# Fused attention and gated layer on one core: Q and K of the last batch by casting transfers from GpSimd, transposed in 64x64 quarters

## The chip, the cores and the metric

The kernel runs on one core of a Trainium2 chip. A core has five engines that run side by side, each working through its own instructions in order: TensorE (PE, matrix products and transposes, with PEld its weight loads), VectorE (DVE), ScalarE (ACT), GpSimd (POOL) and SyncE (SP, which here only issues transfers). Sixteen DMA engines move data between the memory of the device and the on-chip buffers. The metric is device time in microseconds (us) of one execution; a time is the median of the runs shown. One further execution is taken by the hardware profiler, and all lines of profiles and traces below come from such an execution.

## The reference

Batch 8, 8 heads, 576 positions, head dimension 64; everything float32. Attention has a causal mask and a decay bias made of a running sum, and its output goes through a gated layer with a causal convolution of five taps (`x` is the attention output with its heads side by side, `xp` the same with four rows of zeros ahead):

```python
scores = scale * np.matmul(q, k.transpose(0, 1, 3, 2))
s_pos = np.maximum(s, 0.0)
cum = np.cumsum(s_pos, axis=-1)
bias = -(cum[:, :, :, None] - cum[:, :, None, :])
scores = np.where(causal, -1000000000.0, scores + np.minimum(bias, 0.0))
...
attn = np.exp(scores)
attn = attn / (np.sum(attn, axis=-1, keepdims=True) + 1e-09)
return np.matmul(attn, v).astype(np.float32)
...
for k in range(K):
    gate_pre += conv_w[k][None, None, :] * xp[:, k:k + S, :]
gate = 1.0 / (1.0 + np.exp(-gate_pre))
val = x @ w_val
return (gate * val @ w_out).astype(np.float32)
```

## The kernel before

The work is cut into 32 units n = 4 b + p: batch b (0 to 7) and pair p of heads (0 to 3). One unit goes through these steps, each named in the kernel by a short word and the unit's number:

- `s0`, `s1`, `s2`: scores of the pair in blocks (PE, line 506), each followed by its exponential `e0`, `e1`, `e2` (ACT, line 557). `s4`, `e4` do the last 64 positions for a whole batch.
- `mk`: for some units the causal mask of the diagonal blocks, on POOL (line 580); for the others PE does it.
- `vp`: the values of a pair times their decay weights, on POOL (line 475), from the loaded values `vst`.
- `av0`, `av`: the weighted sums of the two heads, PE (line 595). They read the masked exponentials and `vp`'s result. Then `rec`, `nm` (DVE) divide, `xt` (PE) transposes, `xe` copies out.
- `p2` to `p4`, `t1` to `t4`: the convolution taps (POOL lines 655 and 674, DVE, some on ACT), `th` the tanh (ACT), `val` and `out` the two products of the layer (PE, lines 704 and 724), `glu`, `oe` on DVE and ACT, `st` the store (SP).

Q and K come in once a batch, in two halves. In spite of its name, `ld_q.b` brings heads 0 to 3 of both Q and K, and `ld_k.b` heads 4 to 7 of both. Each is two transfers of 512 KB, one of Q and one of K (line 436), into a float32 buffer `qkf`: an even partition 2x holds rows 8x to 8x+7 of Q for four heads, the odd one beside it the same rows of K. `c_q.b` and `c_k.b` (line 374, POOL in most batches) cast a half to bfloat16 into one of three buffers `qkb` and change the order within a partition from (head, row, d) to (row, head, d), so that two heads of a row lie side by side. `qq.b.0` and `qq.b.1` (PE, line 630) then transpose a half in 32 pieces of 64 partitions by 128 columns (two heads), which land in two banks of PSUM with the two heads in the two halves of the partitions; `qe` copies them to `QKT`, from which the scores are formed. Tails of 64 positions come separately (`ld_t`, `tt`, `te`).

No scheduler decides the order. A table, `ORDER`, written out by hand, lists every step as `name:engine:buffers`; the program records the steps in that order, each on the named engine, so each engine's own order is the order of its entries. Semaphores between engines are set by the data and the buffers. An engine whose next instruction has to wait holds back everything behind it.

Around the change the table stands in batches 4 and 5 of attention: units 16 to 20, while Q and K of batches 6 and 7 are brought in. `ld_q.7` uses `qkf` buffer 4 and `ld_k.7` buffer 2, both issued by SP; `c_q.7:G:2` and `c_k.7:G:0` (G is POOL) cast them into `qkb` buffers 2 and 0. `qq.7.0` and `qq.7.1` stand later, among units 21 to 23.

Of the kernel before, what the change touches and what calls it, by code (L numbers as in the profile page):

```python
# [245 lines left out]
xe.16:A s1.18:T:3+4 glu.12.1:V val.13.0:T:7 ld_k.7:S:2 e4.5.3:A glu.12.0:V mk.18:G t1.16:V:0 val.13.1:T:6 e1.18:A  # L246
s2.18:T:1+2 glu.13.1:V vp.5.0:G val.15.0:T:0 e2.18:A t3.16:V s0.19:T:3+4:2 val.15.1:T:6 glu.13.0:V st.0.8:S th.15:A:4
vp.5.1:G t4.16:V av0.18:T:1+2 ld_t.7:S e0.19:A av.18:T glu.15.1:V c_q.6:G:1 rec.18:V s1.19:T:6+7 glu.15.0:V
s2.19:T:3+4 e1.19:A nm.18:V out.1.4:T:0 t2.16:V e2.19:A xt.18:T:1 ld_v.6.0:S vp.5.3:G s0.20:T:6+7:1 xe.18:V tt.6:T:5
e0.20:A oe.1.4:V:1 qq.6.1:T:4:3 mk.19:G t1.18:V:2 th.16:A:1 st.1.3:S av0.17:T:6+7 te.6:V av.17:T qe.6.3:A c_q.7:G:2  # L250
ld_v.6.3:S qq.6.0:T:0:2 rec.17:V qe.6.2:A nm.17:V out.1.6:T:5 t3.18:V qe.6.0:A ld_v.6.4:S av0.19:T:6+7 p2.18:G:1
oe.1.6:V:5 s2.20:T:3+4 xt.17:T:0 e2.20:A t4.18:V mk.20:G av.19:T ld_v.6.2:S out.1.5:T:5 xe.17:V qe.6.1:A rec.19:V
t2.18:G t1.17:V:1 s0.21:T:3+4:0 oe.1.5:A:0 nm.19:V s1.20:T:1+2 st.1.5:S out.1.8:T:5 c_k.7:G:0 e1.20:A ld_v.6.1:S
t2.17:V xt.19:T:6 e0.21:A st.1.2:S out.1.7:T:7 t4.17:V st.1.1:S oe.1.8:A:4 vp.5.2:G xe.19:V s2.21:T:3+4 s1.21:T:1+2
t3.17:V e2.21:A val.16.0:T:5 t1.19:V:3 p3.19:G:0 val.16.1:T:0 ld_v.7.3:S e1.21:A val.17.0:T:3 glu.16.0:V ld_v.7.4:S
glu.16.1:V val.18.0:T:4 p4.19:G:1 th.17:A:2 st.1.4:S t2.19:V s0.22:T:0+1:2 qq.7.0:T:2:5 e0.22:A st.1.6:S glu.17.0:V
t4.19:G val.18.1:T:6 qe.7.0:V val.17.1:T:3 ld_v.7.2:S th.18:A:3 av0.21:T:0+1 oe.1.7:A:0 mk.22:G glu.18.1:V av.21:T
qe.7.1:A ld_v.7.0:S glu.17.1:V s0.23:T:6+7:0 glu.18.0:V t3.19:G s2.22:T:2+3 rec.21:V ld_v.7.1:S e0.23:A av0.20:T:4+5
nm.21:V av.20:T st.1.7:S e2.22:A vp.6.3:G s4.6.3:T:6+7 rec.20:V xt.21:T:0 nm.20:V val.19.0:T:1 th.19:A:0 vp.6.1:G
s1.22:T:2+3 e4.6.3:A glu.19.0:V val.19.1:T:4 e1.22:A xe.21:V xt.20:T:1 glu.19.1:V p3.21:G:1 s1.23:T:6+7 xe.20:V  # L260
p4.21:A:0 s2.23:T:4+5 out.2.2:T:2 t1.20:V:0 e1.23:A vp.6.2:G t1.21:V:1 out.2.1:T:3 e2.23:A t3.20:V vp.6.0:G
qq.7.1:T:6:7 oe.2.1:A:3 t2.21:V av0.22:T:4+5 oe.2.2:A:2 st.2.1:S av.22:T t4.20:V qe.7.3:A t3.21:G out.2.3:T:0 rec.22:V
t2.20:V qe.7.2:A s0.26:T:2+3:1 t4.21:G nm.22:V tt.7:T:1 th.20:A:4 out.2.0:T:6 te.7:V e0.26:A vp.7.0:G oe.2.3:V:1
xt.22:T:7 oe.2.0:A:5 s2.26:T:4+5 xe.22:V s0.24:T:2+3:2 st.2.3:S e2.26:A av0.23:T:0+1 st.2.0:S t1.22:V:2 p4.22:G:1
av.23:T st.2.2:S e0.24:A st.1.8:S s0.25:T:4+5:0 rec.23:V p2.22:G:0 nm.23:V e0.25:A s1.24:T:2+3 t3.22:V xt.23:T:6
mk.24:G e1.24:A s1.25:T:0+1 xe.23:V s2.24:T:4+5 val.20.0:T:7 t2.22:G t1.23:V:3 e1.25:A val.21.0:T:2 glu.20.0:V
val.21.1:T:3 th.21:A:1 t2.23:V val.20.1:T:7 t4.22:G e2.24:A glu.21.0:V s2.25:T:0+1 glu.21.1:V val.22.0:T:2 e2.25:A
t3.23:V vp.7.2:G s1.26:T:4+5 val.22.1:T:3 glu.20.1:V th.22:A:2 t4.23:V av0.25:T:0+1 vp.7.1:G e1.26:A av.25:T
glu.22.0:V s0.27:T:6+7:0 rec.25:V glu.22.1:V e0.27:A s2.27:T:4+5 vp.7.3:G nm.25:V av0.26:T:2+3 av.26:T e2.27:A
xt.25:T:6 mk.27:G rec.26:V av0.24:T:0+1 nm.26:V xe.25:A av.24:T th.23:A:3 p4.25:G:0 t1.25:V:0 s4.7.3:T:4+5 s1.27:T:2+3  # L270
e4.7.3:A val.23.0:T:7 rec.24:V t2.25:V e1.27:A xt.26:T:4 val.23.1:T:5 nm.24:V t4.25:G xe.26:A av0.27:T:2+3 glu.23.1:V
p3.25:A:1 xt.24:T:0 t1.26:V:1 av.27:T xe.24:A out.2.8:T:1 t3.25:G glu.23.0:V p4.26:A:0 t1.24:V:2 out.2.5:T:7
oe.2.8:A:0 rec.27:V t4.26:G t2.24:V th.25:A:0 u0.28:T:5+6:1 oe.2.5:A:3 nm.27:V out.2.6:T:1 f0.28:A p4.24:G:1 st.2.5:S
t3.24:V xt.27:T:7 oe.2.6:A:1 u1.28:T:2+3 u0.29:T:5+6:2 chk0:V xe.27:A st.2.6:S out.2.7:T:1 f1.28:A t1.27:V:3 t4.24:G
out.2.4:T:0 f0.29:A t2.26:V oe.2.7:A:5 val.25.0:T:2 p2.27:G:0 oe.2.4:A:2 t3.27:V av.28.0:T:3 st.2.7:S th.24:A:1
u1.29:T:4+5 st.2.8:S u0.30:T:0+1:0 glu.25.0:V st.2.4:S p3.26:G:1 val.24.0:T:6 t4.27:V f0.30:A val.24.1:T:2 rec.28.0:V
# [5 lines left out]
xe.30.0:A glu.26.1:V u3.29:T:6+7 u2.30:T:4+5:1 t1.30.0:V:3 f3.29:A out.3.2:T:2 t3.29.0:G rec.31.0:V rec.28.1:V
t2.30.0:V f2.30:A out.3.1:T:6 ml.29:G nm.31.0:V oe.3.2:A:4 p4.30.0:G:1 t3.30.0:V xt.31.0:T:7 th.28.0:A:3 st.3.2:S
u3.30:T:2+3 xe.31.0:V p4.29.0:G:0 u2.31:T:4+5:2 f3.30:A nm.28.1:V av.29.1:T:0 t1.31.0:V:1 ml.30:G val.28.0:T:1 f2.31:A
t4.30.0:G rec.29.1:V t3.31.0:V xt.28.1:T:2 val.30.0:T:3 glu.28.0:V xe.28.1:A t4.29.0:G oe.3.1:A:3 av.30.1:T:4
nm.29.1:V p2.28.1:A:1 t4.31.0:V st.3.1:S val.29.0:T:0 th.30.0:A:1 p4.28.1:G:0 t1.28.1:V:0 th.29.0:A:0 t2.31.0:V
u3.31:T:5+6 t2.28.1:G out.3.3:T:1 f3.31:A rec.30.1:V glu.29.0:V t4.28.1:G nm.30.1:V th.31.0:A:4 xt.29.1:T:7 ml.31:G
val.31.0:T:0 glu.30.0:V xe.29.1:A t3.28.1:V xt.30.1:T:4 p3.29.1:G:1 av.31.1:T:3 glu.31.0:V xe.30.1:A th.28.1:A:2
out.3.0:T:2 t1.30.1:V:3 t1.29.1:V:2 rec.31.1:V t3.30.1:V t3.29.1:G out.3.4:T:0 oe.3.0:A:1 nm.31.1:V p2.30.1:G:0
t2.29.1:V oe.3.3:A:5 xt.31.1:T:2 t4.30.1:V out.3.6:T:3 xe.31.1:A t4.29.1:V st.3.3:S t2.30.1:G oe.3.4:A:0 t1.31.1:V:1  # L290
# [4 lines left out]
"""


def main_path(ctx, tc, q, k, v, s, moe_w_val, moe_conv_w, moe_w_out, out, okcnt):
# [129 lines left out]
    def ld_qk(which):  # L428
        def f(e, b, part=None):
            if b == 0:  # L430
                e.dma_start(out=first[part][which],
                               in_=(q, k)[which][0, HP[part], 0:512, :].rearrange("h (p j) d -> p h (j d)", j=4))
                return
            f, hs = halfof(which, b, part)
            for w, src in enumerate((q, k)):
                e.dma_start(out=f.rearrange("(x w) (h e) -> w x h e", w=2, h=4)[w, :, hs],  # L436
                               in_=src[b, 4 * which:4 * which + 4, 0:512, :][hs].rearrange("h (x j) d -> x h (j d)",
                                                                                          j=8))
        return f
# [401 lines left out]
```

## Time and profile before

| what | value |
|---|---|
| median of 3 runs | 190.05 us (189.24 to 191.22) |
| the profiled execution: its own time | 190.71 us |
| its span, first to last instruction | 189.0 us |
| engine busy: PE, DVE, ACT, POOL | 171.9, 164.2, 171.1, 163.6 us |
| POOL casts of a half of Q and K, 128x2048 | 1.89 us each |
| transposes at line 630, all batches from 1 on | 448, PE busy 9.0 us |
| moved by the DMA engines | 40.46 MB, mean 214 GB/s |

The span covers the engines' instructions; the 1.7 us between it and the execution's own time lie around it. Busy times of different engines overlap, since they run side by side. A matmul shows some 190 ns because its pipeline is long, but many are in flight; how fast they follow each other is read from the start times of groups. Instructions that issue transfers are not counted as busy.

### The profile page before, as it was taken

To read this page: it belongs to the slowest core of one execution; us is meant where nothing else is said; L and a number is where in the kernel's file an instruction comes from. 1 tells how busy PE (TensorE), PEld (TensorE's weight loads), DVE (VectorE), ACT (ScalarE), POOL (GpSimd) and SP (SyncE) were. 2 spreads that over 40 slices of the span, in tenths; PEclk is the share of its full clock that TensorE was granted. 3 is DMA by queue.
4 is the path that set the end of the run, shared out by engine and by line. 5 is a ranking of instruction groups with operands and counts; after the bars stand their busy time and mean duration, and the time that the engine had idled before them with its cause. 6 is when DMAs were issued, how large, how long until landed. Compare 5 with 4: busy or idle time off the path is not lost.

```text
span 189.0 us, 6654 instructions
## 1 busy us (share of the span) xinstructions
PE 171.9 (91%) x2720; PEld 113.4 (60%) x2720; DVE 164.2 (87%) x321; ACT 171.1 (91%) x231; POOL 163.6 (87%) x148
## 2 busy tenths in 40 slices
PE   6898785889999998999888999999999999999991
PEld 2556563277747765576564667486566865776560
DVE  4475999669998899999899899998989899999980
ACT  2789899879999999999979998999999999999772
POOL 5467999699999899999969999999999989899620
PEclk9999998799999999999999999999999999999999
DMA  5999889899999999998799999999132003401164
GB/s 176 272 280 267 229 293 207 215 330 343 275 197 342 269 296 252 329 315 223 167 232 260 351 395 231 175 305 249 63 132 93 3 0 114 169 5 55 61 222 173
DMA packets 62283, 40.46 MB, mean 214 GB/s; under 512 B 47333, under 2 KB 49381, under 8 KB 62250
## 3 DMA queue, kind: packets, MB, share of 16 engines
q1 hardware_dynamic: 61706, 39.49, 75.4%
q8 instruction: 22, 0.36, 0.9%
q10 hardware_dynamic: 544, 0.52, 0.8%
q14 instruction: 11, 0.09, 0.2%
HBM read 30.57 MB, written 9.44 MB: 212 GB/s over the span
## 4 chain that ended last, share of the span: by engine, by line
PE 49%; ACT 14%; SPq 13%; DVE 9%; DMA 6%; issue 5%; POOL 2%; ACTq 0%; DVEq 0%; POOLq 0%
PE bank L724 12%; PE bank L704 11%; PE bank L595 10%; ACT P L557 9%; PE bank L506 7%; SPq L472 4%; PE bank L627 3%; SPq L436 3%; DMA vst<-in_v_dram 3%; DMA first<-in_k_dram 3%; PE bank L630 3%; DVE glu L713 3%; ACT th L691 2%; DVE gp L671 2%; DVE xn L614 2%
## 5 line engine op out<-in xcount | busy, mean ns | idle before, releaser
L557 ACT ACTIVATE P<-bank 128x1024 bf16<-128x1024 f32 x84 | 82.9, 1042 | 5.1 <-PE bank L506 3.8
L671 DVE SCALAR_TENSOR_TENSOR gp<-bank,cwr,gp 128x574 f32<-128x574 bf16 (+6 forms) x72 | 52.5, 743 | 0.4
L674 POOL TENSOR_TENSOR gp<-gp,pr 128x572 f32<-128x572 f32 (+6 forms) x36 | 44.9, 1256 | 6.2 <-DVE gp L671 3.3
L475 POOL TENSOR_TENSOR Vp<-vst,w 128x650 bf16<-128x650 f32 x32 | 40.5, 1283 | 2.9 <-DMA vst<-in_v_dram 1.9
L506 PE MATMUL bank<-QKT 64*128 64x128 bf16 (+4 forms) x592 | 38.0, 239 | 4.9 <-ACT P L557 2.2
L704 PE MATMUL bank<-xT,wv 128*128 128x288 bf16 (+2 forms) x256 | 38.5, 287 | 1.0 <-ACT P L557 0.5
L595 PE MATMUL bank<-Vp,P 128*128 128x65 bf16 x960 | 36.0, 194 | 3.2 <-POOL Vp L475 1.0
L595 PEld LDWEIGHTS <-P 128*128 128x128 bf16 x960 | 33.1, 98 | 7.6 <-issue 3.0
L724 PE MATMUL bank<-wo,glu 128*128 128x512 bf16 x144 | 35.8, 380 | 0.2 <-DVE glu L713 0.2
L506 PEld LDWEIGHTS <-QKT 64*128 64x128 bf16 x592 | 19.7, 95 | 22.7 <-issue 15.4
L655 POOL TENSOR_TENSOR pr<-xT,cwr 128x572 f32<-128x572 bf16 (+6 forms) x28 | 28.2, 1015 | 1.6 <-DVE xT L374 0.9
L713 DVE SCALAR_TENSOR_TENSOR glu<-th,bank 128x288 bf16<-128x288 f32 (+2 forms) x64 | 27.7, 447 | 1.9 <-ACT th L691 0.9
L704 PEld LDWEIGHTS <-wv 128*128 128x128 bf16 x256 | 22.4, 97 | 10.9 <-issue 4.8
L614 DVE TENSOR_TENSOR xn<-bank,recs 128x640 bf16<-128x640 f32 (+2 forms) x36 | 26.9, 746 | 0.6
L666 DVE SCALAR_TENSOR_TENSOR gp<-xT,cwr,bank 128x576 f32<-128x576 bf16 (+2 forms) x36 | 26.4, 741 | 0.7
L374 ACT COPY QKT<-bank 128x1024 bf16<-128x1024 bf16 (+1 forms) x26 | 24.1, 970 | 2.6 <-PE bank L490 2.3
L580 POOL TENSOR_SCALAR_AFFINE_SELECT P<-P 128x1024 bf16<-128x1024 bf16 (+1 forms) x22 | 21.3, 972 | 3.9 <-ACT P L557 3.9
L691 ACT ACTIVATE th<-gp,cwr 128x576 f32<-128x576 f32 x28 | 22.0, 792 | 0.2 <-DVE gp L671 0.2
L724 PEld LDWEIGHTS <-glu 128*128 128x128 bf16 x144 | 12.3, 98 | 13.1 <-issue 1.6
L374 ACT COPY ot<-bank 128x512 f32<-128x512 f32 x26 | 15.2, 608 | 1.8 <-PE bank L724 1.0
L627 PE MATMUL bank<-ident,xn 128*128 128x128 bf16 x164 | 15.2, 223 | 0.5 <-ACT P L557 0.3
L608 DVE RECIPROCAL recs<-bank 128x10 f32<-128x10 f32 (+2 forms) x36 | 7.5, 209 | 8.4 <-PE bank L595 7.8
(66 smaller groups left out, 183.3 us busy)
## 6 DMA issues: line engine op xcount, KB each, us to landing
out_dram<-ot SPq DMA_DIRECT2D x36, 256.0 KB, 4.0
vst<-in_v_dram SPq DMA_DIRECT2D x28, 256.0 KB, 5.7
first<-in_q_dram SPq DMA_DIRECT2D x6, 512.0 KB, 4.5
first<-in_k_dram SPq DMA_DIRECT2D x6, 512.0 KB, 6.0
qkf<-in_q_dram SPq DMA_DIRECT2D x6, 512.0 KB, 7.3
qkf<-in_k_dram SPq DMA_DIRECT2D x6, 512.0 KB, 7.3
vst<-in_v_dram SPq DMA_DIRECT2D x15, 128.0 KB, 5.3
first<-in_q_dram SPq DMA_DIRECT2D x4, 256.0 KB, 4.8
```

The costliest lines, as they stand in the source:

```text
L374: (act.copy if e is act else e.tensor_copy)(dst, src)
L475: e.tensor_tensor(Vps[b % 2][:, :, HP[p]], vslot(b)[:, :, HP[p]], w[:, :, b * 8 + 2 * p:b * 8 + 2 * p + 2].unsqueeze(3).to_broadcast([128, ...
L506: pe.matmul(ps[:, hh, c0:c0 + nq], QKTs[b % 2][r, 1, p, k0:k0 + 128], QKTs[b % 2][r, 0, p, q0:q0 + nq], **kw)
L557: act.activation(out=Pt(n)[:, :, step * 512:(step + 1) * 512], in_=pair((f"s{step}", n)), func=AF.Exp, scale=0.125)
L595: pe.matmul(ps[:, o:o + 65], lhsT, Vps[b % 2][:, kb, 2 * p + w, :], start=(kb == 0), stop=(kb == qb))
L614: vec.tensor_tensor(xns[b % 2][:, g, p * 128:(p + 1) * 128].rearrange("t g (w d) -> t w g d", w=2), ps[:, :, :, 0:64], recs[:, n, :, g].un ...
L655: pool.tensor_tensor(pr, xTs[b % 2][:, c, 4 + lo - m:4 + hi - m], r.to_broadcast([128, hi - lo]), ALU.mult)
L671: vec.scalar_tensor_tensor(gp[:, lo:hi], xps(n, *h)[:, lo - m:hi - m], r, gp[:, lo:hi], ALU.mult, ALU.add)
L674: pool.tensor_tensor(gp[:, lo:hi], gp[:, lo:hi], prs[at[f"p{m}", n, *h][0]][:, lo:hi], ALU.add)
L704: pe.matmul(ps, wv[:, dc, c * 128:(c + 1) * 128], xTs[b % 2][:, dc, 4 + lo:4 + hi], start=(dc == 0), stop=(dc == 3))
L713: vec.scalar_tensor_tensor(glu2[:, c, o + lo:o + hi], th[:, lo:hi], 1.0, ps, ALU.add, ALU.mult)
L724: pe.matmul(bank_of(u, i), glu2[:, c, i * 128:i * 128 + 128], wo[:, c, :], start=(c == 0), stop=(c == 3))
```

## The change

For batch 7 alone, the two halves of Q and K are no longer loaded by SP as float32 and cast by POOL. POOL itself issues four transfers (two for each half) that read float32 and write bfloat16 straight into `qkb`. Steps `c_q.7` and `c_k.7` are gone, and so are SP's four transfers. The transfer leaves the order within a partition as it was loaded, (head, row, d), so two heads of a row no longer lie side by side; for these two halves the transposes take pieces of 64 partitions by 64 columns (one head), 64 of them a half where there were 32.

```diff
-t4.12:V vp.4.1:G s2.17:T:1+2 ld_q.7:S:4 out.1.3:T:3 e2.17:A rec.16:V t3.12:V c_k.6:G:0 th.13:A:0 nm.16:V s0.18:T:1+2:1
+t4.12:V vp.4.1:G s2.17:T:1+2 out.1.3:T:3 e2.17:A rec.16:V t3.12:V c_k.6:G:0 ld_q.7:G:2 th.13:A:0 nm.16:V s0.18:T:1+2:1
...
@@ def ld_qk
-            f, hs = halfof(which, b, part)
+            f, hs = (qkb(which, b), slice(0, 4)) if e is pool else halfof(which, b, part)
...
@@ def qk_T2(e, b, h):
+        if (h, b) in by_pool:
+            src = qkb(h, b).rearrange("p (m j d) -> p m j d", m=4, j=8)
+            for p in range(2):
+                for j in range(8):
+                    for r in range(2):
+                        rows = slice(64 * r, 64 * r + 64)
+                        for hh in range(2):
+                            pe.transpose(row_bank(b, h, r)[64 * hh:64 * hh + 64, p * 512 + j * 64:p * 512 + j * 64 + 64],
+                                         src[rows, 2 * p + hh, j, :], ident[rows, rows])
+            return
...
@@ the loop over ORDER
+    by_pool = set()
...
+                if e == "G":
+                    key = ("qkb", "qk".index(f[3]), ix[0])
+                    by_pool.add(key[1:])
```

In the table, `ld_q.7:G:2` now stands right behind `c_k.6`, and `ld_k.7:G:0` behind `qq.6.1` and ahead of `mk.19`; all other entries keep their order.

On POOL, from `c_k.6` to `c_k.7`, before the change. In these rows `qkb0`, `qkb1` and `qkb2` are the three bfloat16 buffers, `Vp` is written by `vp`, `P` by the masks (the first `P1` row is unit 18, `P2` unit 19, the second `P1` row unit 20), `pr` and `gp` belong to the taps:

```order
L374 CAST qkb0_102<-first_91 128x4x8x64
L475 TENSOR_TENSOR Vp0_109<-vst0_92,w_140 128x5x130
L580 AFFINE_SELECT P1_117<-P1_117 128x2x512
L475 TENSOR_TENSOR Vp1_110<-vst1_93,w_140 128x5x130 x2
L374 CAST qkb1_103<-first_91 128x4x8x64
L475 TENSOR_TENSOR Vp1_110<-vst1_93,w_140 128x5x130
L580 AFFINE_SELECT P2_118<-P2_118 128x2x512
L374 CAST qkb2_104<-qkf2_138 128x4x8x64
L655 TENSOR_TENSOR pr1_135<-xT0_113,cwr_144 128x574
L580 AFFINE_SELECT P1_117<-P1_117 128x2x512
L674 TENSOR_TENSOR gp2_121<-gp2_121,pr1_135 128x574
L374 CAST qkb0_102<-qkf0_136 128x4x8x64
```

The same place of POOL after the change (line numbers differ by a few, since the file grew and the table shrank by a line):

```order
L373 CAST qkb0_102<-first_91 128x4x8x64
L435 DMA qkb2_104<-in_q_dram 64x4x512
L435 DMA qkb2_104<-in_k_dram 64x4x512
L474 TENSOR_TENSOR Vp0_109<-vst0_92,w_140 128x5x130
L579 AFFINE_SELECT P1_117<-P1_117 128x2x512
L474 TENSOR_TENSOR Vp1_110<-vst1_93,w_140 128x5x130 x2
L373 CAST qkb1_103<-first_91 128x4x8x64
L474 TENSOR_TENSOR Vp1_110<-vst1_93,w_140 128x5x130
L435 DMA qkb0_102<-in_q_dram 64x4x512
L435 DMA qkb0_102<-in_k_dram 64x4x512
L579 AFFINE_SELECT P2_118<-P2_118 128x2x512
L664 TENSOR_TENSOR pr1_135<-xT0_113,cwr_144 128x574
```

The first pair of issues stands ahead of the mask of unit 18, the second ahead of the mask of unit 19; the two casts stood behind both masks and are gone.

On SP, before the change, the four loads among stores of the output (`out_0`) and the tails of batch 7 (`tail1`); `first` is the buffer of `ld_q.6`:

```order
L436 DMA first_91<-in_k_dram 64x4x512
L459 DMA tail0_105<-in_q_dram 64x8x64
L459 DMA tail0_105<-in_k_dram 64x8x64
L732 DMA out_0_dram<-ot1_129 128x512
L436 DMA qkf2_138<-in_q_dram 64x4x512
L436 DMA qkf2_138<-in_k_dram 64x4x512
L732 DMA out_0_dram<-ot5_133 128x512
L436 DMA qkf0_136<-in_q_dram 64x4x512
L436 DMA qkf0_136<-in_k_dram 64x4x512
L732 DMA out_0_dram<-ot0_128 128x512
L459 DMA tail1_106<-in_q_dram 64x8x64
```

And after it:

```order
L435 DMA first_91<-in_k_dram 64x4x512
L458 DMA tail0_105<-in_q_dram 64x8x64
L458 DMA tail0_105<-in_k_dram 64x8x64
L741 DMA out_0_dram<-ot1_129 128x512
L741 DMA out_0_dram<-ot5_133 128x512
L741 DMA out_0_dram<-ot0_128 128x512
L458 DMA tail1_106<-in_q_dram 64x8x64
```

The stores and the tails behind the four loads move up; nothing else on SP changes. ACT and DVE keep their rows. PE has 128 rows more, all in `qq.7.0` and `qq.7.1`.

More of the change, by code (lines that the diff above doesn't have):

```diff
@@ L247 @@
[L247 to L276, printed above, removed]
@@ L282 @@
[L282 to L286, printed above, removed]
@@ L292 @@
-oe.3.6:A:2 out.3.5:T:1 glu.29.1:V t3.31.1:V st.3.6:S glu.30.1:V val.31.1:T:0 th.31.1:A:1 outa.3.8:T:7 oe.3.5:A:4
-glu.31.1:V chk:V out.3.8:T st.3.5:S outa.3.7:T:0 oe.3.8:A:3 out.3.7:T st.3.8:S cnt:T:7 oe.3.7:A:5 cntc:V st.3.7:S
-flag:S
+xe.16:A s1.18:T:3+4 glu.12.1:V val.13.0:T:7 e4.5.3:A glu.12.0:V mk.18:G t1.16:V:0 val.13.1:T:6 e1.18:A s2.18:T:1+2
+glu.13.1:V vp.5.0:G val.15.0:T:0 e2.18:A t3.16:V s0.19:T:3+4:2 val.15.1:T:6 glu.13.0:V st.0.8:S th.15:A:4 vp.5.1:G
+t4.16:V av0.18:T:1+2 ld_t.7:S e0.19:A av.18:T glu.15.1:V c_q.6:G:1 rec.18:V s1.19:T:6+7 glu.15.0:V s2.19:T:3+4 e1.19:A
@@ new lines @@
+nm.18:V out.1.4:T:0 t2.16:V e2.19:A xt.18:T:1 ld_v.6.0:S vp.5.3:G s0.20:T:6+7:1 xe.18:V tt.6:T:5 e0.20:A oe.1.4:V:1
+qq.6.1:T:4:3 ld_k.7:G:0 mk.19:G t1.18:V:2 th.16:A:1 st.1.3:S av0.17:T:6+7 te.6:V av.17:T qe.6.3:A ld_v.6.3:S
+qq.6.0:T:0:2 rec.17:V qe.6.2:A nm.17:V out.1.6:T:5 t3.18:V qe.6.0:A ld_v.6.4:S av0.19:T:6+7 p2.18:G:1 oe.1.6:V:5
+s2.20:T:3+4 xt.17:T:0 e2.20:A t4.18:V mk.20:G av.19:T ld_v.6.2:S out.1.5:T:5 xe.17:V qe.6.1:A rec.19:V t2.18:G
+t1.17:V:1 s0.21:T:3+4:0 oe.1.5:A:0 nm.19:V s1.20:T:1+2 st.1.5:S out.1.8:T:5 e1.20:A ld_v.6.1:S t2.17:V xt.19:T:6
```

51 lines of the change are left out of this document (40 added, 11 removed).

## The prediction

> **What bounds the kernel now.** I read the page first, then busy time by stretch, the chain of waits, and at the place of the change the timelines of POOL, PE and SP. The engines' line and the stretches (busy us of PE, PEld, DVE, ACT and POOL with instruction counts, granted clock, DMA share, GB/s):
>
> ```profile
> PE 171.9 (91%) x2720; PEld 113.4 (60%) x2720; DVE 164.2 (87%) x321; ACT 171.1 (91%) x231; POOL 163.6 (87%) x148
> 105.00:120.00 15.00, 14.69 (x265) 9.87 (x263) 14.03 (x28) 14.31 (x19) 14.81 (x13) 1.00 1.08 305
> 120.00:138.00 18.00, 17.96 (x289) 11.81 (x289) 16.71 (x31) 17.77 (x24) 17.13 (x14) 1.00 0.71 188
> 138.00:150.00 12.00, 11.53 (x196) 8.17 (x195) 10.99 (x22) 11.96 (x15) 11.92 (x11) 1.00 0.25 90
> ```
>
> All four working engines are nearly full from 105 to 150 us, so the order of handovers decides, not one engine's load. The chain that ended last, around the two batch-7 transposes (start, length, what):
>
> ```profile
> 120.04 1.02 PE bank L724 x4
> ...
> 124.81 0.33 PE bank L506 x8
> 125.14 0.47 PE bank L630 x32
> ...
> 134.30 0.57 PE bank L630 x32
> ...
> 137.91 0.90 ACT P L557
> ```
>
> From 120 to 138 us the chain runs through PE, the two groups of 32 transposes (`qq.7.0`, `qq.7.1`) among it; at 137.9 it passes to ACT, which in 138 to 150 is busy 11.96 of 12 us. Time added to PE here has no idle time to vanish in.
>
> POOL, from `c_k.6` on. The rows are `c_k.6`, `vp.4.2`, the mask of unit 18, two `vp`, `c_q.6`, `vp.5.3`, the mask of unit 19, `c_q.7`; later `c_k.7`, `vp.5.2` and a tap of unit 19:
>
> ```profile
> 103.21 1.89 POOL L374 CAST qkb<-first 128x2048 bf16<-128x2048 f32 x1
> 105.06 1.28 POOL L475 TENSOR_TENSOR Vp<-vst,w 128x650 bf16<-128x650 f32 x1
> 106.29 1.10 POOL L580 TENSOR_SCALAR_AFFINE_SELECT P<-P 128x1024 bf16<-128x1024 bf16 x1
> 107.35 2.53 POOL L475 TENSOR_TENSOR Vp<-vst,w 128x650 bf16<-128x650 f32 x2
> 109.81 1.90 POOL L374 CAST qkb<-first 128x2048 bf16<-128x2048 f32 x1
> 111.66 1.29 POOL L475 TENSOR_TENSOR Vp<-vst,w 128x650 bf16<-128x650 f32 x1
> 112.90 1.10 POOL L580 TENSOR_SCALAR_AFFINE_SELECT P<-P 128x1024 bf16<-128x1024 bf16 x1
> 113.94 1.90 POOL L374 CAST qkb<-qkf 128x2048 bf16<-128x2048 f32 x1
> ...
> 119.53 1.89 POOL L374 CAST qkb<-qkf 128x2048 bf16<-128x2048 f32 x1
> ...
> 125.20 1.40 POOL L674 TENSOR_TENSOR gp<-gp,pr 128x572 f32<-128x572 f32 x1 [0.34 <-DVE gp L671]
> ```
>
> No gap stands in POOL from 103 to 116 us. What PE does with POOL's results, in its own timeline: `av0.18` and `av.18`, then `qq.6.1`, `qq.6.0`, `av0.19`; and `qq.7.0` and `qq.7.1`, each with the group behind it:
>
> ```profile
> 109.01 1.07 PE L595 MATMUL bank<-Vp,P 128*128 128x65 bf16 x30
> ...
> 113.07 0.64 PE L630 MATMUL bank<-ident,qkb 64*128 64x64 bf16 x32
> 113.73 1.07 PE L595 MATMUL bank<-Vp,P 128*128 128x65 bf16 x30
> 114.73 0.64 PE L630 MATMUL bank<-ident,qkb 64*128 64x64 bf16 x32
> ...
> 116.18 0.61 PE L595 MATMUL bank<-Vp,P 128*128 128x65 bf16 x15
> ...
> 124.98 0.63 PE L630 MATMUL bank<-ident,qkb 64*128 64x64 bf16 x32
> 125.54 1.15 PE L704 MATMUL bank<-xT,wv 128*128 128x288 bf16 x8
> ...
> 134.24 0.64 PE L630 MATMUL bank<-ident,qkb 64*128 64x64 bf16 x32
> 134.81 1.08 PE L595 MATMUL bank<-Vp,P 128*128 128x65 bf16 x30
> ```
>
> **The casts.** Two go: 1.90 + 1.89 = 3.79 us of POOL. Nobody waited for them: `c_q.7` ended at 115.84 and is read at 124.98, `c_k.7` at 121.42 and 134.24. In 95 to 150 us POOL itself waits, and is waited for, this much (total, times, longest):
>
> ```profile
> POOL gp L674 <- DVE gp L671: 2.2, 4, 1.5
> PEld L630 <- POOL Vp L475: 0.4, 1, 0.4
> ```
>
> POOL behind the casts stops for DVE already (the 0.34 us at 125.20), so arriving there earlier only lengthens that stop. I cost the removal as no gain, but as room in which POOL catches up after 114 us.
>
> **The four issues on POOL.** No row shows POOL issuing a transfer, so I bound it by SP's issues of the same four transfers and by POOL's own pass over the same half:
>
> ```profile
> 103.51 0.61 SPq L436 DMA_DIRECT2D qkf<-in_q_dram  x1
> 104.17 0.67 SPq L436 DMA_DIRECT2D qkf<-in_k_dram  x1
> 105.59 1.30 SPq L436 DMA_DIRECT2D qkf<-in_q_dram  x1
> 106.93 0.66 SPq L436 DMA_DIRECT2D qkf<-in_k_dram  x1
> ```
>
> SP takes 0.61 to 0.67 us for three of them (the 1.30 is beside full DMA engines). POOL needs 1.89 us to touch every element of a half. Issuing must name 256 rows a transfer (64 partitions, 4 heads), more than nothing and less than every element. Neither end is nearer in kind, so I take the middle, 1.25 us an issue, 2.5 a pair, 5.0 for both; zero (the issue stays beside POOL's work) to 1.9 stays in the range.
>
> The Trainium skill, "DMA: Bandwidth & Descriptors", section "Specifications", puts the first byte of a GpSimd transfer at about 1 us against 0.6 us for SP; SP's issue rows of 0.61 us are of the second's size, though an issue is not a first byte, and no run here shows the first. By 1 us an issue, an estimate from that page, the stall below would be 1.8 us and the sum 193.0.
>
> Behind the first pair wait `vp.4.2` and the mask of unit 18, both read by the `av` pair at 109.01. The mask ended at 106.29 + 1.10 = 107.39: slack 1.62 us. A pair of 2.5 us makes PE wait 2.5 - 1.62 = 0.88 us. `c_q.6` would end 2.5 us after 111.71, at 114.21, still ahead of its reader at 114.73. The second pair waits for `qq.6.1` (its buffer is read by it), which ends at 113.73 before and at 114.6 with the delay; POOL arrives at 112.95 + 2.5 = 115.4, so that wait costs nothing. Behind it waits the mask of unit 19, which ended at 114.00 and is read by `av0.19` at 116.18: slack 2.18. With 5.0 us the mask is done 2.82 us late for PE, the first 0.88 counted in it. Behind `av0.19` on PE stand the scores of unit 20 and all that follows; ACT waited for PE in this stretch already, so its own rows move too and I let the full 2.82 us reach the end. After that POOL is 5.0 - 1.90 = 3.1 us late at the tap product behind `c_q.7` and 1.2 us behind `c_k.7`, with PE itself 2.82 late: no second stall.
>
> **The quarters.** `qq.7.0` takes 125.54 - 124.98 = 0.56 us, `qq.7.1` 134.81 - 134.24 = 0.57: 17.7 ns a piece. Now 64 pieces each. If a piece keeps its pace, each group grows by 0.57, together 1.13 us on PE in the chain; if four quarters run side by side as two halves may do now, nothing; if they run singly, at twice 17.7 ns, 64 x 35.4 = 2.27 us, or 1.7 more a group, 3.4 in all. I take 1.13, because the rows give a pace by instruction and the instruction count doubles.
>
> Here the Trainium skill speaks the other way: "TensorEngine Tiling (Array Packing)", section "Tiling Modes", lets the four 64x64 tiles load and multiply independently. By that rule the 1.13 is nothing and the sum is 192.9; the rows cannot show it, as none has 64 columns of weights.
>
> **SP and the transfers.** SP loses four issues (0.61 + 0.67 + 1.30 + 0.66 = 3.24 us); stores and value loads behind them may leave earlier, but no POOL row above stops for a load, so I give it nothing. The landing time of the two halves before:
>
> ```profile
> DMA to landing us min/median/max: 8.1/8.2/8.2
> ```
>
> The first pair is issued by 107.6 us and would land by 116, nine before 124.98; the second by 118 and 126, eight before 134.24. Writing half the bytes could shorten this, casting on the way lengthen it; either hides.
>
> **The sum.** Against the profiled execution's own 190.71 us: + 2.82 + 1.13 = 194.66. That execution lies 0.66 above the median of 190.05, so on the scale of the medians 190.05 + 3.95 = 194.0 us.
>
> **The rivals.** *A, no change worth the name:* an issue costs POOL little and PE's quarters overlap. Up to 0.5 us an issue no mask is late (4 x 0.5 = 2.0 under 2.18); then 190.05 to 191.2 us. For it: the masks' slacks. Against it: SP's 0.61 us. The Trainium skill's section "Anatomy of one DMA" on the DMA page calls descriptor generation "small, variable", which would be this case.
>
> *B, faster:* POOL sets the pace of 97 to 150 us, unseen because the other engines lean on it through short handovers. Then 3.79 us less of casting counts, at most 190.05 - 3.79 + 1.13 = 187.4 with free issues. It decides only below (3.79 - 1.13 - 1.9) / 4 = 0.19 us an issue. For it: POOL at 14.81 of 15 us. Against it: both masks wait over 1.6 us for their reader, and the only waits for POOL come to 0.4 us.
>
> *C, much slower:* issues beyond 1.9 us, or pieces that run singly: 4 x 1.9 - 2.18 = 5.4, with 1.13 to 3.4 that is 196.6 to 198.9 us.
>
> **Chances.** What a measurement of this kernel can tell from no change is about 1%, 1.9 us. My forecast 0.56 (it needs more than (1.9 - 1.13 + 2.18) / 4 = 0.74 us an issue), A 0.27, B 0.10, C 0.07. Slower by over 1%: 0.56 + 0.07 = 0.63. The low end takes in A whole with 0.25 us for scatter, 189.8; the high end stands at the foot of C with 0.4 more, 197.0; B and the upper part of C stay out.
>
> **What would show it.** Right: in the changed profile, gaps on PE ahead of the `av` groups of units 18 and 19 whose releaser is POOL's mask, together near 2.8 us, POOL without recorded work for some 2.5 us ahead of each of those masks, and line 642 with 64 pieces in 1.1 us. A is right if both masks start within 2 us of their old places and PE shows no such gap; B if the rows behind 121 us all start earlier. My prediction is wrong if the wait falls elsewhere: at `qq.7.1` for a landing (the transfer is slow), or at the second pair for `qq.6.1`.

## The result and the profile after

The changed kernel takes 191.84 us (median of 12 runs, 191.15 to 192.52) against 189.95 us (189.15 to 191.23): a ratio of 1.010, with a 95% interval of 1.0073 to 1.0126, or 1.9 us slower (1.4 to 2.4). The forecast was 194.0, 3.95 us slower. The ratios leave disturbed runs out, so that in some experiments the ratio lies below the quotient of the medians. The profiled execution took 192.33 us with a span of 190.2 (before: 190.71 and 189.0).

POOL from the issues to the second mask, and two later rows (timeline of POOL, changed kernel: start, length, engine and line, operation, output<-input; in brackets the idle time ahead and what ended it):

```profile
104.93 0.81 POOL L435 DMA_DIRECT2D qkb<-in_q_dram  x1
105.74 0.62 POOL L435 DMA_DIRECT2D qkb<-in_k_dram  x1
106.37 1.30 POOL L474 TENSOR_TENSOR Vp<-vst,w 128x650 bf16<-128x650 f32 x1
107.61 1.09 POOL L579 TENSOR_SCALAR_AFFINE_SELECT P<-P 128x1024 bf16<-128x1024 bf16 x1
...
114.21 0.68 POOL L435 DMA_DIRECT2D qkb<-in_q_dram  x1
114.88 0.62 POOL L435 DMA_DIRECT2D qkb<-in_k_dram  x1
115.50 1.11 POOL L579 TENSOR_SCALAR_AFFINE_SELECT P<-P 128x1024 bf16<-128x1024 bf16 x1
...
122.17 2.24 POOL L664 TENSOR_TENSOR pr<-xT,cwr 128x573 f32<-128x573 bf16 x2 [0.82 <-DVE xT L373]
125.35 1.40 POOL L683 TENSOR_TENSOR gp<-gp,pr 128x572 f32<-128x572 f32 x1 [0.94 <-DVE gp L680]
```

An issue takes POOL 0.62 to 0.81 us, four of them 2.73. The profile records POOL's issues as work of its own, unlike SP's, so no stretch without recorded work stands there. The mask of unit 18 starts 1.32 us later than before (107.61 for 106.29), that of unit 19 2.60 later (115.50 for 112.90). Behind the place of the two casts, POOL now waits 0.82 and 0.94 us for DVE (before: 0.34 at the second of these rows), so the casting time it is spared turns into waiting.

PE at the readers of the two masks and at the quarters (timeline of PE, changed kernel):

```profile
108.90 1.07 PE L594 MATMUL bank<-Vp,P 128*128 128x65 bf16 x30
...
115.20 1.04 PE L733 MATMUL bank<-wo,glu 128*128 128x512 bf16 x4
116.67 0.63 PE L594 MATMUL bank<-Vp,P 128*128 128x65 bf16 x15 [0.43 <-POOL P L579]
...
119.26 0.40 PE L505 MATMUL bank<-QKT 64*128 64x128 bf16 x8
...
125.22 0.71 PE L642 MATMUL bank<-ident,qkb 64*64 64x64 bf16 x64
125.87 1.15 PE L713 MATMUL bank<-xT,wv 128*128 128x288 bf16 x8
...
134.55 0.71 PE L642 MATMUL bank<-ident,qkb 64*64 64x64 bf16 x64
135.19 1.08 PE L594 MATMUL bank<-Vp,P 128*128 128x65 bf16 x30
```

No gap for unit 18; 0.43 us for the mask of unit 19. A group of 64 quarters holds PE 0.65 and 0.64 us (125.22 to 125.87, 134.55 to 135.19) where 32 pieces held it 0.56 and 0.57. These two things delay PE by about half a microsecond. The last copy of ACT (timeline of ACT, before, then after) starts only 0.38 us later,

```profile
184.90 0.58 ACT L374 COPY ot<-bank 128x512 f32<-128x512 f32 x1 [0.23 <-PE bank L724]
```

```profile
185.28 0.59 ACT L373 COPY ot<-bank 128x512 f32<-128x512 f32 x1 [0.23 <-PE bank L733]
```

while the span is 1.2 longer: most of the loss in this pair of profiles lies behind the last computation. There, the events of SP under the closing condition (SP's first group: the waits for its eight DMA semaphores; second: the closing of the program), of the kernel before,

```profile
L808 SPq EVENT_SEMAPHORE  x8: 17/17/17, 187.0 to 187.6; - x8
L836 SPq EVENT_SEMAPHORE  x10: 17/28/28, 187.7 to 188.9; - x10
```

and after:

```profile
L821 SPq EVENT_SEMAPHORE  x8: 17/17/17, 187.3 to 188.6; - x8
L849 SPq EVENT_SEMAPHORE  x12: 17/28/28, 188.7 to 190.1; - x12
```

Before, six of the eight waits pass while the last store is still on its way; it holds the seventh semaphore and one wait follows its landing (187.56). After, it holds the third, and five waits, 0.066 to 0.083 us apart in the trace, follow its landing (188.27). Two waits more follow in the closing, for POOL's own DMA queue. The last store itself, from its issue to its landing (DMA view of the last 4 us, before, then after):

```profile
out_dram<-ot SPq DMA_DIRECT2D x1, 256.0 KB, 2.0
```

```profile
out_dram<-ot SPq DMA_DIRECT2D x1, 256.0 KB, 2.4
```

And from 183.0 to 186.3 us the changed kernel has a row that the kernel before has not, a fetch of instructions:

```profile
q8 instruction: 1, 0.02, 1.7%
```

Last, the time outside the span (each run's time less its span) is 2.05 us (median of 12 runs, 1.97 to 2.13); of the kernel before it is 1.75 (29 runs beside the first experiments, 1.67 to 1.87). So there are six candidate costs, and the experiments are about their size and cause.

### The profile page after: what moved, and what is told of

Its sections match the earlier page's. It is cut to its first block, busy times and chain, and to the rows that moved or that the text cites. A ratio compares the mean times of both kernels' runs of the same rounds, so it can differ in the third digit from the quotient of the medians.

```text
span 190.2 us, 6783 instructions
## 1 busy us (share of the span) xinstructions
PE 172.2 (91%) x2784; PEld 113.6 (60%) x2784; DVE 163.6 (86%) x321; ACT 171.2 (90%) x231; POOL 162.7 (86%) x150
## 4 chain that ended last, share of the span: by engine, by line
PE 43%; POOL 16%; SPq 11%; DMA 10%; DVE 7%; ACT 6%; issue 4%; POOLq 0%; DVEq 0%; ACTq 0%
PE bank L733 11%; PE bank L713 11%; PE bank L594 9%; DMA vst<-in_v_dram 8%; POOL Vp L474 6%; PE bank L505 6%; POOL qkb L373 5%; SPq L471 5%; ACT P L556 4%; SPq L435 3%; PE bank L626 2%; DVE glu L722 2%; DMA first<-in_k_dram 2%; POOL gp L683 1%; POOL P L579 1%
## 5 line engine op out<-in xcount | busy, mean ns | idle before, releaser
L579 POOL TENSOR_SCALAR_AFFINE_SELECT P<-P 128x1024 bf16<-128x1024 bf16 (+1 forms) x22 | 22.5, 1025 | 4.0 <-ACT P L556 4.0
```

## The experiments

Theory: the loss is a sum of POOL's issues (through the mask of unit 19), the quarters, and costs at the end of the program that come with the change without being its work. Rivals: the issues carry it alone; the quarters carry it; or casting transfers slow the program in some way not yet seen. In the diffs, `:S`, `:G`, `:T` after a step name SP, POOL and PE.

### One tiny transfer from POOL (e1)

```diff
-p2.14:G:0
+p2.14:G:0 tiny.0:G        # e.dma_start(out=spare[0:1, :], in_=moe_conv_w[0:1, 0:64]), float32 to bfloat16
```

> The kernel before with one more transfer of 64 numbers (cast to bfloat16, read by nobody), issued by POOL in its idle time at 95 us; nothing else differs. Theory Q (having a transfer on POOL's own queue at all costs time at the program's end and outside the span): the last 128x512 copy ends where it does before (185.5 us, within 0.2), time minus span rises from 1.71 to about 2.05 us, one more semaphore wait of 0.07 us stands at the end, and the median is 0.4 us above before. Rival S (the end was only scatter of landings, and the changed kernel pays through the mask stall and the quarters alone): median within 0.15 us of before and time minus span 1.7 us.

190.83 us, ratio 1.0015 (0.9981 to 1.0049). The issue (timeline of POOL):

```profile
95.24 0.68 POOL L754 DMA_DIRECT2D spare<-in_moe_conv_w_dram  x1
```

64 numbers cost POOL as much as half a batch's Q or K (0.62 to 0.81): the price belongs to the issue, not to the bytes. The time outside the span rose to 2.11 us (median of 12, 1.70 to 2.21) against 1.75, and the transfer is the only thing added: here the use of POOL's queue brought some 0.3 us. The total time, with 0.4 us expected, cannot resolve it.

### The quarters alone (e2)

```diff
-            copy(e, qkb(which, b).rearrange("p (j h d) -> p h j d", j=8, h=4)[:, hs],
+            if b == 7: copy(e, qkb(which, b), f); return      # straight order, by POOL as before
...
 def qk_T2(e, b, h):
+    if b == 7: (the 64 transposes of the changed kernel)
```

> The kernel before, with SP's loads and POOL's two casts kept, but the casts of batch 7 keep the order (head, row, d) and PE transposes that batch in 64 pieces of 64x64 a half. Theory: each group takes 0.65 us against 0.56, with a pause of up to 0.1 ahead, 0.15 to 0.3 us together on PE, all of it at the end; casts in straight order keep their 1.89 us; time minus span 1.7 us. Median 0.15 to 0.3 above before. Rival (the pieces' pace, as I forecast): 1.13 us above before. Rival (they cost nothing): within 0.1.

190.50 us, ratio 1.0014 (0.9979 to 1.005): within the noise of nothing, and its upper end, 0.95 us, lies below the 1.13 of the prediction. The trace is sharper. PE's rows at 119 us and behind the second group, of this kernel,

```profile
118.89 0.40 PE L509 MATMUL bank<-QKT 64*128 64x128 bf16 x8
...
134.82 1.08 PE L598 MATMUL bank<-Vp,P 128*128 128x65 bf16 x30
```

and of the kernel before at the first of these places (the second, 134.81, is in the prediction):

```profile
119.12 0.40 PE L506 MATMUL bank<-QKT 64*128 64x128 bf16 x8
```

15.93 us for 15.69: the quarters cost 0.24 us. The changed kernel has 135.19 - 119.26 = 15.93, the same, and four later kernels without quarters (e1, e7, e9, e13) have 15.64 or 15.65.

### The issues behind the masks (e3), and twice as many (e4)

```diff
-c_k.6:G:0 ld_q.7:G:2 ... mk.18:G ... ld_k.7:G:0 mk.19:G
+c_k.6:G:0 ... mk.18:G ld_q.7:G:2 ... mk.19:G ld_k.7:G:0                                  # e3
+c_k.6:G:0 ld_q.7:G:2 again.0:G ... mk.18:G ... ld_k.7:G:0 again.1:G mk.19:G              # e4
```

`again` issues the same two transfers once more, into a buffer that nothing reads.

> The changed kernel with each pair of issues moved behind the mask that it stood ahead of (units 18 and 19). Theory: the gap of 0.43 us on PE ahead of the weighted sums of unit 19 goes, the first pair still delays the mask of unit 19 by 1.4 us, inside its slack of 2.18; the last copy ends 0.25 us (0.1 to 0.6) earlier than in the changed kernel, the median falls by as much, from 1.9 to about 1.6 us above before. Rival (the stall carries the loss): the median falls to within 0.5 us of before.

> The changed kernel with each pair of issues made twice, the second into a free buffer that nobody reads: eight issues, 5.4 us of POOL, and 2 MB more read. This is the POOL time that I forecast for four issues (5.0 us). Theory (beyond the slack every us counts once on PE, only the price of an issue was wrong): the mask of unit 18 is late by 2.7 - 1.6 = 1.1 us and that of unit 19 by 5.4 - 2.2 = 3.2 in all; the last copy ends 2.5 to 3.2 us later than before, and the median lies 3.7 to 4.5 us above before. Rival (PE finds the time again further on, since 0.35 of the 0.6 us were found in the changed kernel): the last copy ends under 1.5 us later.

e3: 191.82 us, ratio 1.007 (1.004 to 1.0099). PE waits for neither mask, and 1.3 us of the 1.9 are still there. The rival that the issues, through the masks, carry the loss alone is out.

e4: 195.73 us, ratio 1.027 (1.0217 to 1.0323). POOL spends 5.4 us on eight issues, a little more than the 5.0 that the prediction had for four, and PE's readers of the masks of units 18 and 19 show

```profile
110.23 1.08 PE L594 MATMUL bank<-Vp,P 128*128 128x65 bf16 x30 [0.95 <-POOL P L579]
...
119.34 0.90 PE L594 MATMUL bank<-Vp,P 128*128 128x65 bf16 x15 [1.99 <-POOL P L579]
```

together 2.94 us: the prediction's gaps (0.88 and 2.82 in all) nearly as it drew them, once POOL really has that much to do. Its mechanism is right, its price for an issue wrong. The time, 5.1 us (4.1 to 6.1) above the kernel before, exceeds the 3.7 to 4.5 that was expected. The profiled execution, at 197.12 us the longest of the six, shows two things that add to it. Right behind the wait of 1.99 us the granted clock was half for 3.4 us (stretches of e4: start and end, length, busy us of PE, PEld, DVE, ACT and POOL, granted clock, DMA share, GB/s),

```profile
119.50:122.90 3.40, 3.40 (x42) 2.35 (x40) 1.07 (x3) 1.93 (x2) 3.40 (x4) 0.50 1.22 201
```

and the end of the span is longer (table below).

### SP's semaphores (e5, e7), POOL's idle times (e6, e8)

```diff
+tiny.0:S tiny.1:S ... tiny.2:S tiny.3:S    # e5: in the changed kernel, where the four loads stood; e7: in the
+                                           # kernel before, behind st.1.7 and st.2.1; 64 numbers each, unread
-ld_q.7:G:2 ... ld_k.7:G:0                  # e6 and e8 (e8: with e5's loads)
+p2.14:G:0 ld_q.7:G:2 ... vp.5.2:G ld_k.7:G:0
```

> The changed kernel with four 64-number loads on SP where the four loads of Q and K stood, so that the DMA semaphores rotate again as before; nothing reads what they bring. Theory that part of the loss is the order of the waits at the program's end: the last store's semaphore is again next-to-last of the eight instead of third, five waits of 0.066 us no longer stand behind it, and the time falls by about 0.3 us against the changed kernel (191.84), to 191.5. Rival, that the order at the end is no cost: 191.8. Time outside the span stays at about 2.05 us by both.

> The kernel before with four 64-number loads on SP in its long waits after 130 us, so that the DMA semaphores rotate as in the changed kernel; POOL issues nothing. Theory of the end's order: the last store's semaphore is third of the eight, and the time rises by about 0.3 us (ratio 1.0016). The time outside the span stays at 1.75 us if POOL's queue is what lengthens it, and goes to 2.05 if the rotation does.

> The changed kernel with Q's two issues moved up into POOL's idle time at 95 us (1.40 us) and K's two down into the idle time at 122 us (0.82 us), so that POOL's casts of unit 6 and the masks of units 18 and 19 run as early as in the kernel before or earlier. Theory that POOL's issues reach the end through the mask of unit 19: no wait for a mask at the matmuls of units 18 and 19, and the time falls by the 0.43 us of that wait, to 191.4. Rival, that PE takes the lost time back before 119 us: the wait is gone and the time stays at 191.6 to 191.9, its rest being the quarters (0.25 us) and the program's end.

> Both edits on the changed kernel: issues in POOL's idle times and the four 64-number SP loads. If the loss is the sum of mask wait, quarters, order at the end and POOL's queue, what is left is the quarters (0.25), the queue's two waits and longer clear at the end (0.2) and the time outside the span (0.3): about 0.75 us over the kernel before, ratio 1.004. Rival, that the casting transfers themselves slow the program in a way not yet seen: 1.3 us or more, ratio 1.007 or more.

The kernels take the eight semaphores of SP's transfers in turn, so four transfers more or less move the last store by four places. From the traces (us; "landing" is from the last store's issue to its landing, "to the end" from there to the end of the span):

| kernel | ACT's last copy | landing | to the end | outside the span |
|---|---|---|---|---|
| before | 184.90 | 2.04 | 1.45 | 1.75 |
| before, other rotation (e7) | 183.87 | 2.05 | 1.74 | 1.89 |
| before, one POOL transfer (e1) | 183.95 | 2.03 | 1.56 | 2.11 |
| before, quarters (e2) | 184.91 | 2.44 | 1.45 | 1.71 |
| after | 185.28 | 2.38 | 1.94 | 2.05 |
| after, rotation turned back (e5) | 185.11 | 2.42 | 1.65 | 2.02 |
| after, eight POOL transfers (e4) | 189.43 | 2.43 | 2.80 | 1.80 |

The rotation alone is 0.29 us, added in e7 and taken away in e5; POOL's queue adds 0.20 in the closing (1.65 for 1.45; 0.11 with a single POOL transfer) and 0.3 outside the span. The rotation alone lengthened that too (1.89 in e7), but turning it back did not shorten it (2.02 in e5), so the 0.3 is put down to the queue, as in e1. That is not settled: e4 issues eight transfers from POOL, and its time outside the span is 1.75 to 1.85 in all six runs, as without the queue. Its closing inside the span is 0.86 us longer than that of the changed kernel (2.80 for 1.94), so what the queue costs at the end can lie on either side of the span's last instruction. The 13 profiles with transfers from POOL also show a fetch of instructions behind the end of the span and the five without show none; whether it takes part in the 0.3 us is open.

The times fit, but would not have shown the rotation: e7 190.56, ratio 1.0024 (0.999 to 1.0059); e5 191.93, 1.0093 (1.0059 to 1.0127).

e6 missed both forecasts: 195.52 us, ratio 1.0256 (1.0199 to 1.0313); e8 likewise, 195.21 us, ratio 1.0124 (1.0045 to 1.0204, from two of its six runs). The waits for the masks were gone, but in e6, at 104 to 107 us, DVE and then PE show

```profile
105.99 0.69 DVE L373 COPY ot<-bank 128x512 f32<-128x512 f32 x1 [2.03 <-DMA out_dram<-ot]
```

```profile
106.73 0.19 PE L505 MATMUL bank<-QKT 64*128 64x64 bf16 x1 [1.32 <-DVE ot L373]
```

DVE waited 2.03 us for a store to free its `ot` buffer; in the changed kernel the same copy starts at 104.46 without a wait. The place at 95 us puts a megabyte of reads among stores where the DMA share of the changed kernel, without them, is already 1.09 (95 to 105 us), and a store that somebody waits for comes late. The Trainium skill, "DMA: Bandwidth & Descriptors", section "Issuing engines are not separate DMA queues", says that transfers of all issuing engines interleave on the same 16 DMA engines; this wait agrees.

That wait is not the whole of the miss: the profiled execution of e6 took 193.75 us, less than any of its five other runs. In the profile of e8 the wait of PE at this place is 2.37 us, and behind it the granted clock is again half for 3.4 us:

```profile
107.30:110.70 3.40, 3.40 (x17) 1.46 (x17) 2.19 (x5) 1.36 (x2) 3.40 (x4) 0.50 0.89 289
```

Four of the six runs of e6 have a granted clock of 0.967 to 0.983, against 0.990 and 0.991 in its two shortest; that the same happened there is likely, but those runs have no trace. An idle time of POOL was no free place for a transfer here.

### The last store's landing (e9, e10), and several costs taken back (e11, e12)

In all kernels so far, the landing of 2.4 us appears in every one with quarters and in no other, and with it the fetch of instructions near 184 us. The quarters lengthen TensorE's program by 64 matmuls and 64 weight loads. If that shifts the fetches in time, 64 other matmuls must do the same, and 64 more on top of the quarters must undo it.

```diff
 def unread(e, i):
+    if i in (4, 6):      # two of the 32 unread warm-up matmuls, at 3 to 4 us
+        for j in range(33): pe.matmul(bank[0:64, ...64 columns], ident[0:64, 0:64], ident[0:64, 0:64], ...)
+        return
```

e9 is the kernel before with this, e10 the changed kernel; e12 is e10 with e5's loads, e11 is e12 with the issues behind the masks as in e3.

> The kernel before with two of its 32 unread warm-up matmuls (at 3 to 4 us) replaced by 66 unread ones of 64x64, so that TensorE's program has 64 matmuls and 64 weight loads more, as many as the quarters add; Q and K of the last batch as before. Theory that the longer program moves a fetch of instructions into the last stores: a 16 KB packet of an instruction queue near 183.7 us, the last store landing 2.4 us after its issue instead of 2.05, and the time up by 0.35 us (ratio 1.002). Rival, that the 64x64 transposes themselves or chance make the landing late: it stays at 2.05 us, and the time at that of the kernel before.

> The changed kernel with the same 64 matmuls and weight loads added at 3 to 4 us, so that the fetches of instructions fall where they fell in the kernel before (the last of the 16 KB packets near 175 us). Theory of the fetch: the last store lands 2.05 us after its issue instead of 2.38 and the time falls by 0.35 us, to 191.5. Rival: landing 2.4 us and 191.8.

> The changed kernel with three costs taken back at once: the issues behind the masks, the 64 matmuls at 3 to 4 us, and four 64-number SP loads where the four loads stood. If the costs add up, what is left over the kernel before is the quarters (0.23 us), POOL's queue in the waits and the clear at the end (0.20) and outside the span (0.30): 0.7 us, time 190.9, ratio 1.004. Rival, that a cost is missing from the list: 191.5 or more, ratio 1.007 or more. The rival that POOL's issues cost by the masks alone would have it at 190.2.

> The same without moving the issues: the changed kernel with the 64 matmuls and the four 64-number SP loads. If the wait for the mask of unit 19 costs its 0.25 to 0.45 us, the time is that much above the run with the issues behind the masks, 191.2 to 191.3; if PE takes it back, 190.9. The wait for the mask is back in the trace by both.

All four were slower than expected: 192.83, 193.97, 192.99 and 193.50 us, ratios 1.0142 (1.01 to 1.0184), 1.0193, 1.0154 and 1.0178. The small matmuls themselves are dear so early (PE of e9):

```profile
3.26 1.97 PE L623 MATMUL bank<-ident 64*64 64x64 bf16 x33
```

60 ns each, six times the price of a quarter at 125 us, and the start of the program is 3.7 to 4.1 us late, of which 1.2 to 2.0 us is left at 113 us. So these times stand beside each other, not beside the kernel before. The landing does not depend on that, and decides: 2.45 us in e9, 2.03, 2.02 and 2.01 in e10, e11 and e12. The DMA view of the last store in e10:

```profile
out_dram<-ot SPq DMA_DIRECT2D x1, 256.0 KB, 2.0
```

Over all kernels: 2.03 to 2.05 us in the three with TensorE's program as before, 2.38 to 2.48 in the ten that are 128 instructions longer (two of them without any quarters), 2.01 to 2.03 in the five that are 256 longer. The fetch, 1.8 to 1.9 us ahead of the last store's issue, stands in those ten profiles and in none of the other eight. The cost belongs to the length of TensorE's program and where in it a fetch falls, not to the transposes. The fetch lasts 0.88 us, so it is over before the last store is issued; that it holds up one DMA engine's packets of the stores ahead, and the last store behind them, is the likely way, but was not shown by itself.

e12 and e11 differ by the place of the issues alone and reach 116 us within 0.05 us of each other. PE in e12,

```profile
116.50 1.04 PE L739 MATMUL bank<-wo,glu 128*128 128x512 bf16 x4
118.07 0.63 PE L595 MATMUL bank<-Vp,P 128*128 128x65 bf16 x15 [0.54 <-POOL P L580]
...
120.67 0.40 PE L506 MATMUL bank<-QKT 64*128 64x128 bf16 x8
```

and in e11:

```profile
116.45 1.04 PE L739 MATMUL bank<-wo,glu 128*128 128x512 bf16 x4
117.33 0.62 PE L595 MATMUL bank<-Vp,P 128*128 128x65 bf16 x15
...
119.97 0.40 PE L506 MATMUL bank<-QKT 64*128 64x128 bf16 x8
```

(120.67 - 116.50) - (119.97 - 116.45) = 0.65 us (the medians of the two kernels differ by 0.51): the mask of unit 19 costs 0.65, not the 0.25 that the first two profiles differ by (119.26 - 115.20 for the changed kernel; before, 119.12 - 115.31). The profiled run of the kernel before had lost time of its own there, in the group behind the reader of the mask:

```profile
116.73 0.75 PE L506 MATMUL bank<-QKT 64*128 64x320 bf16 x4
```

0.75 us for a group that takes 0.39 after. Of the other kernels without a late mask, e1, e3, e6 to e9, e11, e13 and e15 lose at most 0.07 there, but e2 loses some 0.6, in the same group:

```profile
116.86 0.39 PE L509 MATMUL bank<-QKT 64*128 64x320 bf16 x3 [0.33 <-ACT QKT L374]
```

A single profile of the kernel before was a poor yardstick for that stretch. e1 and e7 run the same program on TensorE as the kernel before, so the loss changes from execution to execution; its cause is open, and so is how many of the timed runs of the kernel before had it. If all of them had, the mask would cost some 0.3 us less against them.

### The sum once more, with a later filler (e13 to e16)

```diff
 def unread(e, i):
+    if 24 <= i < 28:     # four unread matmuls at 34 to 37 us, ahead of a wait of PE
+        for j in range(17): pe.matmul(... the same 64x64 ...)
+        return
```

e13 is the kernel before with it, e14 the changed kernel with it and e5's loads, e15 the same with the issues behind the masks, e16 the changed kernel as it is.

> The kernel before with four of its unread warm-up matmuls at 34 to 37 us replaced by 68 unread ones of 64x64 (64 matmuls and 64 weight loads more), where TensorE waits for other engines right behind them, so that the start is not delayed as in the run with the small matmuls at 3 to 4 us. Theory of the moved fetch of instructions: last store landing 2.4 us after its issue, time 0.35 us above the kernel before and nothing else changed. Rival, that the fetch is no cost of its own: the time of the kernel before.

> The changed kernel with the same 64 matmuls at 34 to 37 us and the four 64-number SP loads. The landing (0.35) and the order of the end's waits (0.29) are taken back: 0.64 us under the changed kernel of the same job. If the terms do not add up: within 0.3 us of it.

> The same with the issues behind the masks too. The mask of unit 19 costs 0.65 us where the two runs with small matmuls at 3 to 4 us are set side by side, so 1.3 us under the changed kernel, and 0.7 us (quarters 0.23, POOL's queue 0.5) over the kernel before, ratio 1.004. Rival, that something of the change is not on the list: ratio 1.007 or more.

> The changed kernel once more, for a comparison within one job: 1.9 us above the kernel before, ratio 1.010 (1.007 to 1.013), a wait of 0.4 to 0.6 us for the mask of unit 19, last store landing 2.4 us after its issue. A ratio under 1.007 would say that the first measurement was high.

e16: 191.77 us, ratio 1.0086 (1.0058 to 1.0114), so the first measurement holds: 1.6 us (1.1 to 2.2) beside 1.9. The landings came as expected: 2.47 us in e13, 2.03 in e14 and e15, 2.48 in e16.

The times did not settle the sum. e13 192.77, e14 193.79, e15 193.19 (ratios 1.0103, 1.0157 and 1.0084, intervals of 1.1 to 1.2% in width): in most of their runs the granted clock was 0.962 to 0.973, which no run of the kernel before shows in that job (0.978 to 0.991). Runs at a clock of 0.987 or more took 190.42 and 190.56 (e13), 191.41 (e14), 190.51, 190.62, 190.63 and 191.51 (e15). Beside 190.0 that is +0.5, +1.4 and +0.6 (median), where the prices ask for +0.4, +1.4 and +0.7. It fits, but runs picked by their clock after the fact are support and no proof. The profile of e15 (an execution of 194.32 us) shows where the clock went: it is half for 10.2 us around the filler (32.5 to 42.7 us), in the kernel before for 3.4 us (31.6 to 35.0). e14 and e15 also lost 0.28 and 0.57 us inside a group of matmuls behind the first quarters (PE of e14; "issue" is time in which nothing that the profile shows was waited for):

```profile
128.65 0.32 PE L506 MATMUL bank<-QKT 64*128 64x128 bf16 x5 [0.28 <-issue]
```

What was missing there stays open.

No version beat the kernel before. Of the changed ones, e3 is the fastest by its ratio (1.007).

## Why the prediction was half right

The prices, as the experiments leave them:

| term | forecast, us | measured, us | by |
|---|---|---|---|
| wait for the mask of unit 19 | 2.82 | 0.65 | e12 beside e11 |
| quarters | 1.13 | 0.24 | PE from 119 to 135 us, after and e2 |
| last store's landing | 0 | 0.35 to 0.4 | e9, e13 against e10 to e12 |
| order of the end's waits | 0 | 0.29 | e7, e5 |
| POOL's queue in the closing | 0 | 0.20 | after, e5 |
| POOL's queue outside the span | 0 | 0.30 | e1 (not in e4) |
| sum | 3.95 | 2.0 to 2.1 | whole: 1.9 (1.4 to 2.4), again 1.6 (1.1 to 2.2) |

The direction was right; the size was off by half, because the two terms that it had were over four times too large, and four that it did not have made up for part of that. There is luck in the direction: its own two terms, at their measured size, come to 0.9 us, less than the 1.9 that it said could be told from no change. The measured prices come from single profiles; their sum fits both measurements, and so would a mask that costs 0.3 us less, so the times do not prove the list complete.

**The issue's price, the step that failed.** "Neither end is nearer in kind, so I take the middle, 1.25 us an issue" mixed two kinds of work. Issuing the same transfers was what SP did at 0.61 to 0.67 us; touching every element (1.89) is another kind, and e1 shows that the elements do not enter. With the 2.73 us that the four issues took, the prediction's own formula gives 2.73 - 2.18 = 0.55 us for the mask of unit 19, where the traces show waits of 0.43 to 0.60; SP's 0.61 to 0.67 would have given 0.26 to 0.50. The slacks (1.62 and 2.18), the place and the reader were right, and e4 reproduces the gaps at the POOL time assumed. Its own condition, more than 0.74 us an issue, was just missed at 0.68. The profile's window of such an issue, by the Trainium skill ("Perfetto Trace Analysis", section "DMA Instruction — SWDGE (GPSIMD)"), ends when the descriptors are made; that agrees with POOL's next row beginning at that moment.

**The quarters.** That "the rows give a pace by instruction" was the wrong reading: the pace fell from 17.7 to 10.2 ns a piece (0.65 / 64). The rule of the Trainium skill ("TensorEngine Tiling (Array Packing)", section "Tiling Modes"), which the prediction gave against itself, was the nearer one, though the pieces are not free: 0.07 to 0.09 us a group, and 0.24 with what follows.

**What held.** The casts taken from POOL are no gain, their time turned into waits for DVE. The landing is hidden: Q's and K's transfers land a median of 6.8 and 7.9 us after their issue (DMA view of 88 to 125 us, after),

```profile
qkb<-in_q_dram POOLq DMA_DIRECT2D x2, 256.0 KB, 6.8
qkb<-in_k_dram POOLq DMA_DIRECT2D x2, 256.0 KB, 7.9
```

ten and more microseconds ahead of their transposes (125.22 and 134.55), and no second stall came behind 119 us.

**What it had no term for.** Between 1.1 and 1.2 us lie where the change does no work: behind the last copy and outside the span. The "so I give it nothing" on SP was right for the loads and overlooked that four SP transfers less turn the rotation of the semaphores, that POOL's queue must be waited for and cleared at the end, and that a longer TensorE program fetches its instructions at other times. Of these, the rows of before show only the eight waits themselves.

**Rivals.** A (no change) had the cheap issue and the overlapping quarters nearly right, but its 190.05 to 191.2 us fell short for the same missing terms. B was far off: its point of decision was 0.19 us an issue. C needed more than 1.9.

## What to carry to other kernels

Price an operation that a trace does not show by the row of the same kind of work on another engine, not by the middle between unlike rows. With the body of a tuned kernel delayed by under 1 us, read the end of the program too: which semaphore the last store holds, which queues the closing waits for, and what is fetched beside the last transfers. Compare a suspect stretch in several profiles; here one profile of the kernel before hid 0.4 of 0.65 us. Look at the granted clock behind a wait of PE: two waits of about 2 us were each followed by 3.4 us at half clock, which no sum of waits contains.

## What the hardware showed that was not expected

- A transfer issued by POOL held it for 0.62 to 0.82 us, for 64 numbers as for half a batch; one such transfer added about 0.3 us outside the span (e1), while with eight (e4) the span's own end grew instead (2.80 us from the last landing, 1.94 with four).
- 128 more instructions in TensorE's program make the last store land 0.35 to 0.4 us later, 256 more do not: a 16 KB fetch of instructions stands 1.8 to 1.9 us ahead of the last store in the ten profiles of the first kind and in none of the others.
- SP's waits for DMA semaphores at the end cost about 0.07 us each even when fulfilled, so moving the last store by four places among the eight was worth 0.29 us (e7, e5).
- TensorE's waits of 1.99 us (e4) and 2.37 us (e8) were each followed by 3.4 us at a granted clock of 0.50.
- 64x64 matmuls took 60 ns each at 3 us (e9) and transposes of that size 10 ns at 125 us. The view prints a granted clock of 1.00 for both, but the trace of e9 has no clock record before 10.3 us. And 68 of them at 34 to 37 us brought most runs to a lower granted clock (0.962 to 0.973 against 0.978 to 0.991).
